# The first half batch taken unit by unit: v in q's layout, masks as bias matmuls, sink blocks of its own, and four FFN chunks between the units

## The chip, the cores and the metric

The kernel runs on one core of a Trainium2 chip. Its engines work side by side, each on its own list of instructions in a fixed order: TensorE (PE; PEld is its weight load), VectorE (DVE), ScalarE (ACT), GpSimd (POOL) and SyncE (SP), which here only issues transfers. They wait for one another through semaphores. PE writes into eight PSUM banks, P in the listings; all else works in SBUF. The metric is the device time of one execution in microseconds.

## The reference

Attention with a sliding window of 128 tokens and four sink tokens, then a feed-forward network (FFN) on its output. Inputs and output are float32; the kernel computes in bfloat16 and sums in float32.

```
B, H, S, D = 4, 8, 768, 64          # batches, heads, tokens, head size
keep = (key < 4) | ((query - key >= 0) & (query - key < 128))
a    = softmax(where(keep, q @ k.T / 8, -1e9));   o = a @ v
x    = o.transpose(0, 2, 1, 3).reshape(3072, 512)
h    = x @ w_in                     # 512 x 2048
out  = (h * sigmoid(beta * h)) @ w_out   # 2048 x 512
```

A block of 128 queries needs its own 128 keys (diagonal block, d), the 128 before them (previous block, p), and the four sink keys, which lie in key block 0 (s: a block that holds both window and sink).

## The kernel before, in words

The 3072 tokens are eight half batches of 384 (three blocks of 128). A unit is two heads of one half batch, so a half batch has four units. For a unit: q and k are cast to bfloat16 (`cast`), transposed on PE (`T`, six 128 x 128 transposes, then two copies to `qkT`), multiplied to scores (`SC`, in bursts of tiles of four blocks), put through exp on ACT into `E`, masked by multiplication on DVE or POOL, multiplied with v (`AV`; a column of ones in `vaug` gives the sum), divided by that sum (`rden`, `onorm` on DVE), and transposed into `xT` (`OT`). Query blocks from the third on do not see key block 0 through the window; for them the sink keys of all heads lie side by side in `kS`, their scores are one small matmul group (`SS`, exp to `ES`), and their values lie in `vS`, which `AV` multiplies first (line 915). For the first half batch `vS` is picked from `vaug` by a matmul with `sel` (`first_values_pe`, line 680).

A chunk of the FFN, H0 to H15 per half batch (`HQ`), is four matmuls of `w_in16` with the four units' rows of `xT` (line 970), tanh on ACT (line 975) and a product on DVE (line 977); the second layer is `OQ` (line 993). H0 and H1 need the weight tile w0, H2 and H3 w1, H4 to H7 w2 and w3, H8 to H11 w4 and w5, H12 to H15 w6 and w7. Each tile arrives as float32 (`load_w`) and is cast (`cast_w`).

The order is made in Python before anything runs. `Graph` records every operation with its reads and writes, and `arrange` then orders each engine's list by assumed durations, with PE's groups nearly in the order in which they were recorded. Where PE would stand idle in the opening, `fill` puts in matmuls of ones on ones into bank 7 (line 1212), which nobody reads. In the first half batch the recorded order is by hand, with hand-picked banks: all four units' transposes and scores, then sink scores (F) and values (V), then attention (A) and output transposes (R). The FFN of half batch 0 begins with H0 after that, between the transposes T4 to T7 of the second half batch, whose scores are the bursts S5 to S7.

Transfers go out on SP in recorded order; the first k loads go out on ACT. q and k of the first three half batches come three tokens to a partition (768-byte rows); v comes one token to a partition (256-byte rows), so that a block of v has its tokens in order. The order in which the three tokens of q and k stand is undone in the copy to `qkT`.

The lines that matter beside those: 604 (loads of q, k, v), 616 (weights), 534 to 577 (constants on POOL), 523, 525 and 528 (copies and casts on ACT, POOL and DVE), 725 (transposes), 823 (scores), 840 (exp), 848, 854 and 858 (masks), 926 (attention).

## Time and profile before

| | |
|---|---|
| Times of three runs | 221.15, 221.72 and 222.12 us, median 221.72 |
| Span of the profiled execution, first to last instruction | 219.7 us |
| Time of the profiled execution | not listed by itself; the median of the runs is 2.0 us above the span |
| PE busy | 213.4 us, 97% |
| ACT, DVE, POOL busy | 147.2, 138.1 and 75.2 us |
| Matmuls of ones on ones (line 1212) | 35, 11.3 us |
| First FFN matmul (line 970) | at 21.17 us |
| Read from memory, written | 27.37 and 6.29 MB |
| Granted TensorE clock | 1.000 |

In the page's slices each digit is the busy share in tenths of a fortieth of the span (5.5 us). In a group of instructions the figures after the bar are the busy time, the mean duration, and the idle time of the engine just ahead of them with what ended it. Durations of matmuls are modelled to the end of the array, so several in a row overlap; what counts for PE is the step from one to the next.

### The profile page before, as it was taken

The numbers are of one execution on the slowest core, as the hardware profiler recorded it, in microseconds if no ns is written. First come the engines' busy times: TensorE is split into PE (matmuls) and PEld (weight loads), VectorE is DVE, ScalarE is ACT, GpSimd is POOL, SyncE is SP. The second block draws the span as 40 slices with busy tenths as digits, with TensorE's granted clock in tenths as the row PEclk, the third lists the DMA queues.
The fourth block names the chain that finished last, engine by engine and source line by source line (L and its number), as shares of the span: only waits on it lengthen the run. The fifth ranks groups of instructions, "written<-read, shape, count | busy, mean of one in ns | idle before, by whom it ended". The sixth has DMA issues, their size and how long they took to land.

```text
span 219.7 us, 4563 instructions
## 1 busy us (share of the span) xinstructions
PE 213.4 (97%) x1776; PEld 120.8 (55%) x1793; DVE 138.1 (63%) x293; ACT 147.2 (67%) x241; POOL 75.2 (34%) x140
## 2 busy tenths in 40 slices
PE   8999999999999999999999999999999999999995
PEld 3455557555575575446554556446565456465443
DVE  1697899697774278358960788478886248088000
ACT  2698999586975798459865597275886574187211
POOL 7344551112550790067103770184101770100100
PEclk9999999999999999999999999999999999999999
DMA  6999999999989998499837997659949111400122
GB/s 190 240 302 364 357 287 357 371 298 204 226 185 188 225 141 217 92 253 218 196 74 180 228 182 203 139 142 237 136 98 209 40 63 27 144 2 0 51 95 95
DMA packets 94717, 39.86 MB, mean 181 GB/s; under 512 B 82072, under 2 KB 89512, under 8 KB 94696
## 3 DMA queue, kind: packets, MB, share of 16 engines
q1 hardware_dynamic: 91928, 33.28, 68.9%
q0 software_dynamic: 1680, 5.51, 7.5%
q10 hardware_dynamic: 1088, 0.79, 1.1%
q8 instruction: 14, 0.23, 0.5%
q14 instruction: 7, 0.06, 0.1%
HBM read 27.37 MB, written 6.29 MB: 153 GB/s over the span
## 4 chain that ended last, share of the span: by engine, by line
PE 88%; DVE 6%; DMA 3%; ACT 2%; issue 1%; ACTq 0%
PE P L993 38%; PE P L970 36%; PE P L926 5%; PE P L823 4%; DMA k_stage<-in_k_dram 3%; DVE E L858 2%; PE P L725 2%; PE P L952 1%; DVE g L977 1%; PE P L915 1%; DVE E L848 1%; PE P L870 1%; PE P L1212 1%; DVE w_in L528 1%; ACT E L840 0%
## 5 line engine op out<-in xcount | busy, mean ns | idle before, releaser
L970 PE MATMUL P<-xT,w_in 128*128 128x384 bf16 x512 | 86.8, 327 | 0.4 <-ACT w_in L523 0.2
L993 PE MATMUL P<-w_out,g 128*128 128x512 bf16 (+2 forms) x383 | 84.6, 371 | 1.0 <-issue 0.2
L975 ACT ACTIVATE t<-P,hbeta 128x384 f32<-128x384 f32 x128 | 72.4, 590 | 17.6 <-PE P L970 11.0
L977 DVE SCALAR_TENSOR_TENSOR g<-t,P 128x384 bf16<-128x384 f32 x128 | 67.9, 550 | 21.1 <-ACT t L975 15.7
L970 PEld LDWEIGHTS P<-xT,w_in 128*128 128x128 bf16 x512 | 49.0, 98 | 33.4 <-DVE g L977 0.8
L993 PEld LDWEIGHTS P<-w_out,g 128*128 128x128 bf16 x400 | 37.3, 98 | 40.5 <-issue 0.5
L840 ACT ACTIVATE E<-P 128x1024 bf16<-128x1024 f32 x44 | 43.1, 1036 | 14.1 <-PE P L823 14.1
L854 POOL TENSOR_SCALAR_AFFINE_SELECT E<-E 128x512 bf16<-128x512 bf16 x59 | 38.8, 684 | 27.4 <-ACT E L840 27.2
L1011 POOL DMA_DIRECT2D out_dram<-osb x21 | 11.8, 562 | 63.5 <-ACT osb L523 63.5
L523 ACT ACTIVATE osb<-P 128x512 f32<-128x512 f32 x14 | 8.4, 597 | 25.1 <-PE P L993 25.0
L932 DVE TENSOR_TENSOR onorm<-P,rden 128x384 bf16<-128x384 f32 x32 | 17.6, 554 | 0.8
L529 DVE TENSOR_SCALAR osb<-P 128x512 f32<-128x512 f32 x9 | 6.2, 688 | 15.0 <-PE P L993 14.9
L848 DVE TENSOR_TENSOR E<-E,maskS 128x512 bf16<-128x512 bf16 x16 | 8.8, 564 | 10.4 <-ACT E L840 10.4
L926 PE MATMUL P<-vaug,E 128*128 128x65 bf16 x352 | 15.0, 193 | 0.0
L926 PEld LDWEIGHTS P<-vaug,E 128*128 128x128 bf16 x352 | 14.0, 97 | 1.4 <-ACT E L840 0.4
L823 PEld LDWEIGHTS P<-qkT 64*128 64x128 bf16 x288 | 9.5, 94 | 7.6 <-issue 4.3
L823 PE MATMUL P<-qkT 64*128 64x128 bf16 (+1 forms) x288 | 13.2, 230 | 0.1
L1212 PE MATMUL P<-ones 128*128 128x512 bf16 (+1 forms) x35 | 11.3, 446 | 1.1 <-POOL ones L534 1.1
L528 DVE CAST vaug<-v_stage 128x512 bf16<-128x512 f32 x19 | 9.5, 509 | 3.2 <-DMA v_stage<-in_v_dram 3.1
L697 POOL TENSOR_TENSOR kS<-qkT,headm 128x8 bf16<-128x8 bf16 (+1 forms) x10 | 2.5, 251 | 17.7 <-DMA qkT<-k 9.5
L915 PE MATMUL P<-vS,ES 128*128 128x130 bf16 x40 | 8.1, 221 | 0.4 <-DVE vS L682 0.4
L525 POOL TENSOR_SCALAR_AFFINE_SELECT q<-q_stage 128x512 bf16<-128x512 f32 x7 | 4.8, 693 | 10.4 <-DMA q_stage<-in_q_dram 10.4
(64 smaller groups left out, 119.6 us busy)
## 6 DMA issues: line engine op xcount, KB each, us to landing
v_stage<-in_v_dram SPq DMA_DIRECT2D x24, 256.0 KB, 4.8
out_dram<-osb POOLq DMA_DIRECT2D x21, 256.0 KB, 3.6
q_stage<-in_q_dram SPq DMA_DIRECT2D x15, 256.0 KB, 4.8
k_stage<-in_k_dram SPq DMA_DIRECT2D x15, 256.0 KB, 4.9
wst<-in_moe_w_in_dram SPq DMA_DIRECT2D x5, 512.0 KB, 8.3
wst<-in_moe_w_out_dram SPq DMA_DIRECT2D x4, 512.0 KB, 8.1
g<-in_moe_w_out_dram SPq DMA_DIRECT2D x4, 512.0 KB, 6.6
q_stage<-in_q_dram SPq DMA_DIRECT2D x2, 768.0 KB, 7.8
```

Of the source, the lines that this page charges most:

```text
L528: return lambda e: e.tensor_copy(dst, src)
L823: add("pe", lambda e, dst=dst, kt=kt, kc=kc, rows=rows, q0=q0, nq=nq, u=u: e.matmul(dst, kt[rows, kc:kc + 128], qkT[rows, u % NT, 0, q0:q0 ...
L840: add("act", lambda e, src=src, dst_=dst_: e.activation(dst_, src, AF.Exp, bias=0.0, scale=SCALE), act_ns(1024), w=[("E", z)] + [("m", z, ...
L854: alts = {"gp": (lambda e, dd=dd, sg=sg: e.affine_select(dd, dd, [[0, 4], [sg, 128]], ALU.is_ge, 0.0, base=min(sg, 0), channel_multiplier= ...
L926: e.matmul(A[:, c0:c0 + D + 1], E[t_ % NE][:, i, hh, :], vaug[vz][:, kb % NK, 2 * hp + hh, :], start=a, stop=o, skip_group_check=True), 31,
L932: add("dve", lambda e: e.tensor_tensor(onorm[on][:, :, :, :].rearrange("p m h d -> p (m h) d"), av[:, :, 0:D], rden[on][:, :].unsqueeze(2) ...
L970: add("pe", lambda e, c=c: e.matmul(hp, w_in16[:, c, m * 128:(m + 1) * 128], xT[:, c, t0:t0 + HALF], start=(c == 0), stop=(c == 3)), mm_ns ...
L975: add("act", lambda e: e.activation(tt[ti][:, :], hp, AF.Tanh, bias=0.0, scale=hbeta[:, m:m + 1]), act_ns(HALF) + 93, r=["hbeta"], w=[("t" ...
L977: add("dve", lambda e: e.scalar_tensor_tensor(gt[T_ % NG][:, m, :], tt[ti][:, :], 1.0, hp, ALU.add, ALU.mult), dve_ns(HALF), r=[("t", ti)] ...
L993: add("pe", lambda e, m=m: e.matmul(P[:, bk, 0:n], gt[T_ % NG][:, m, t * 128:(t + 1) * 128], w_out16[:, m, cols], start=(m == 0), stop=(m ...
L1011: add(eng, lambda e: e.dma_start(out_t[3 * T_ + t], osb[z][:, :]), 262144 / 300, r=[("osb", z)], dma=f"do{eng}{z}", hold={"sp": 550, "gp": ...
L1212: G.fill([lambda e, n=n: e.matmul(P[:, 7, 0:128 * n].rearrange("p (a b) -> p a b", a=n), ones[:, :], ones[:, :].unsqueeze(1).to_broadcast( ...
```

## The change

What it does, part by part, for the first half batch only unless said otherwise:

- v is loaded like q and k, three tokens to a partition, by unit. POOL casts it into `vmix` (`mix`); nine matmuls per unit with 0/1 matrices `onehot` (`sort`) put its tokens in order into a bank, and a copy brings it to `vaug`. The 0/1 matrices are built on POOL at the start, in buffers `osb0` and `osb1`; `vmix` lies in the buffer `g1`.
- The masks are no longer multiplied into `E`. Ahead of the score matmuls, matmuls of the identity with `biasS`, `biasT` or `biasX` write 0 or -30000 into the bank, and the scores are added to that (`EARLY` is 4 in place of 0).
- Each unit has two tiles: one of four blocks (s s d d), and one of two blocks, p and a new kind x: key block 0 against query block 2 with all keys but the sink keys masked. So `SS`, `sel`, `first_values_pe` and the `vS` matmuls go for these units. `vS` for the second half batch comes from a small transfer (`load_first`) and is multiplied on POOL.
- The recorded order is by unit (`ENTRY`). H0 to H3 are computed in four parts (`HP`): as soon as a unit's `xT` is there, its one of the four matmuls of each of the four chunks is issued into four banks that stay held until the fourth unit.
- Transfers: the first loads go in the order of `LOAD0`; then come beta, w0 and w1, q and k of the second half batch, w3, w2, w5, w4, its three v tiles, w6 and w7 (`FIRST`).
- After the opening, PE's recorded order follows the string `ORDER`, with a look ahead of eight entries, in place of the rule-based choice. Banks are chosen by the planner, not by hand.
- The planner's assumed stalls and some assumed durations are changed, and an operation that may go to several engines is given, while it is recorded, to the one with the earliest free slot.

```diff
+ENTRY = "T0 S0 V0 T1 S1 V1 T2 S2 A0 A1 V2 V3 A2 R0 T3 S3 R1 P0 A3 B R2 P1 R3 P2 P3"
+FIRST = "w0 w1 q k w3 w2 w5 w4 v1 v2 v0 w6 w7"
+ORDER = "THHTTTHASHHHSHHSHAHHHAHHOROHOHHRHAHRTROHOAOHSORTOSOOATHOTHHOOHHHOSOHHOHOHRAAARAOHRROSOOHHHAHSOOHHOOHAHHRHHROHRHOROOSRAOOSOOOOHHOHAARHHHHAHOHRHHHHHHOHOOSOOHOHHOOHHSOHOHHHHHHROHHOARSAORHRAORAOOOSOAOROOHHHHHHHHROHOHHHHHHHHRHHHHHHHHOOOOOSOOOOOHHSHHHARHOOHHHHROOHOOOHOOHRRHHHOOHHOHOHOHHOOOOOOOOOOOOOOOOH"
...
+LOAD0 = "q0 k0 v0 q1 k1 v1 k3 k2 s q2 v3 v2 q3"
+LOOK, AHEAD_W = 4, 8
...
-        self.stalls = [(16000.0, 1100.0), (34000.0, 700.0)]
+        self.stalls = [(4900.0, 900.0), (14000.0, 700.0), (27000.0, 500.0), (36000.0, 500.0)]
...
-    EARLY, BST, SOON = 0, [1,2,2]+[3]*5, 2200
+    EARLY, BST, SOON = 4, [1,2,2]+[3]*5, 2200
...
+        for j in range(NK):
+            add("gp", lambda e, j=j: e.affine_select(
+                onehot[j].rearrange("p (a w) -> p a w", w=128), ones[:, :].unsqueeze(1).to_broadcast([128, NK, 128]),
+                [[-128, NK], [-1, 128]], ALU.is_equal, 0.0, base=j, channel_multiplier=NK), 520,
+                r=["ones"], w=[("pick", j), ("osb", j // 2)])
...
-        if n == "v" or hb >= CUT:
+        if n == "v" and hb == 0:
+            hs = slice(2 * i, 2 * i + 2)
+            src = v[b, hs, t0:t0 + HALF, :].rearrange("h (p j) d -> p h (j d)", j=NK)
+            dst, keys, ns = v_p[:, hs, :, :].rearrange("p h j d -> p h (j d)"), [("stv", i)], NQ0
+        elif n == "v" or hb >= CUT:
...
+    def mix(i):
+
+        hs = slice(2 * i, 2 * i + 2)
+        any_of(copies(vmix[:, hs, :], v_p[:, hs, :, :].rearrange("p h j d -> p h (j d)"),
+                      {"gp": 520}), r=[("stv", i)], w=[("vmix", i)], lock=True)
+
+    def sort(i):
+
+        G.begin()
+        bk = take(1)
+        hs = slice(2 * i, 2 * i + 2)
+        for c in range(NK):
+            for j in range(NK):
+                add("pe", lambda e, c=c, j=j: e.matmul(
+                    P[:, bk[0], 128 * c:128 * c + 128], onehot[j][:, c * 128:(c + 1) * 128], vmix[:, hs, j * D:(j + 1) * D],
+                    start=j == 0, stop=j == NK - 1), mm_ns(128), r=[("pick", j), ("osb", j // 2), ("vmix", i)],
+                    x=[("B", bk[0])])
+        any_of(copies(vaug[0][:, :, hs, 0:D], P[:, bk[0], 0:HALF].rearrange("p (c h d) -> p c h d", h=2, d=D),
+                      {"act": 380, "dve": 465}),
+               r=[("vones", 0)], w=[("v", 0, c, i) for c in range(NK)], x=[("B", bk[0])])
+        give(bk)
...
-        add("dve", lambda e: e.tensor_tensor(
+        add("dve" if b else "gp", lambda e: e.tensor_tensor(
             vS[z][:, :, 0:D], vS32[:, 0:1, :].to_broadcast([128, H, D]),
...
+        if hb == 0:
+            return [t for i in range(4) for t in (
+                [("s", i, 0, 0), ("s", i, 0, 1), ("d", i, 1, 1), ("d", i, 2, 2)], [("p", i, 1, 2), ("x", i, 0, 2)])]
...
+                               "px": [(0, biasPX)]}[kinds]:
+                    dst = bank[:, a:min(a + 2, len(kinds)), :]
+                    add("pe", lambda e, dst=dst, src=src, a=a: e.matmul(
+                        dst, ident[:, :], src, start=a == 0, stop=False, skip_group_check=True), mm_ns(128 * min(2, len(kinds))),
...
-            far = NK * half + m >= 2
+            far = NK * half + m >= 2 and u >= EARLY
...
+    def HP(c):
+        G.begin()
+        if c == 0:
+            for m in range(4):
+                first_h.extend(take(1))
+        for m in range(4):
+            HQ(0, m, [first_h[m]], [c])
...
-    for x in "T0:63 T1:01 S1:01 T2:64 T3:46 S0:12 S4:56 S3:34 S2:01 F:2 V:5 A1:1 A0:5 A2:4 R0:5 A3:2 R1:0 R2:4 R3:0".split():
...
+    for x in ENTRY.split():
+        i = int(x[1:] or 0)
+        if x[0] == "V":
+            sort(i)
...
+        elif x[0] == "P":
+            HP(i)
+            if i == 3:
+                give(first_h)
...
-    early = "H0 T4 H1 H2 H3 T5 H4 T6 T7 H5 S5 H6 H7 H8 H9 S6 H10 H11 S7 H12 H13 H14".split()
...
+    todo, idle_ = list(ORDER), 0
     while True:
         background()
         now = G.free["pe"]
+        if todo:
...
+            for pos, x in enumerate(todo[:AHEAD_W + 4 * max(0, idle_ - 8)]):
```

In the letters of the orders, T is a transpose group, S a score burst, V a sort, A attention, R an output transpose, P a quarter of H0 to H3, B beta, H a chunk, O a quarter of a second-layer tile.

More of the change, by code (lines that the diff above doesn't have):

```diff
@@ L214, in arrange @@
                     t = max(self.free[e], ready(o, e), self.shut(o, e))
[L215 removed]
+                    if o.dma and o.chain != 0:
                         t = max(t, self.dma_free - 3000)
@@ L603, in load @@
         after = [("stg", n, z, j) for j in range(4)] if hb in range(CUT, CUT + NSTG) and n != "v" else ()
+        if hb == 2 and n == "v":
+            after = [("stv", j) for j in range(4)]
         add("act" if hb == 0 and n == "k" and Q2 else "sp", lambda e: e.dma_start(dst, src), ns, w=keys,
@@ L645, in cast @@
             r, w = [("stb", n, z, i), ("vones", hb % NV)], [("v", hb % NV, i)]
+            w += [("v", 0, i, j) for j in range(4)] if hb == NV else []
         elif hb == 0:
@@ L790, in SC @@
         tiles, first = BURSTS[n]
+        assert all(t_ < NE or SPAN[t_ - NE][1] < done["AV"] for t_ in tiles)
         bs = take(2 * len(tiles))
@@ L973, in HQ @@
                 r=w_keys(m) + [("xT", c, T_ % NXT)], x=[("B", bs[0])])
-        spare_ = [("wst", NWS // 2 + z) for z in range(NWS // 2)] if (T_, m) == (NG - 1, 0) else []
+        if cs[-1] < 3:
+            return
+        ti = hi[0] % NTT
+        hi[0] += 1
+        spare_ = [("vmix", i) for i in range(4)] if T_ == 1 and m < 4 else []
+        spare_ += [("wst", NWS // 2 + z) for z in range(NWS // 2)] if (T_, m) == (NG - 1, 0) else []
         add("act", lambda e: e.activation(tt[ti][:, :], hp, AF.Tanh, bias=0.0, scale=hbeta[:, m:m + 1]),
```

254 lines of the change are left out of this document (143 added, 111 removed).

## The prediction

> **What bounds the kernel now.** I read the page first (who is busy, and in which slices), then the sums by stretch, then the chain of work in order of time, then the timeline of the first 37 us. The page:
>
> ```profile
> span 219.7 us, 4563 instructions
> PE 213.4 (97%) x1776; PEld 120.8 (55%) x1793; DVE 138.1 (63%) x293; ACT 147.2 (67%) x241; POOL 75.2 (34%) x140
> ...
> PE   8999999999999999999999999999999999999995
> ...
> L1212 PE MATMUL P<-ones 128*128 128x512 bf16 (+1 forms) x35 | 11.3, 446 | 1.1 <-POOL ones L534 1.1
> ```
>
> PE is nearly always busy, but 11.3 us of that are L1212, matmuls of ones on ones that nobody reads. All of them lie in the opening, so only the opening has PE time to give. The busy time by stretch (start:end, length, then PE, PEld, DVE, ACT, POOL, clock, DMA share, GB/s):
>
> ```profile
> 5.30:21.20 15.90, 14.32 (x163) 8.36 (x162) 12.56 (x31) 12.74 (x23) 6.50 (x18) 1.00 1.06 298
> 21.20:24.20 3.00, 3.00 (x24) 1.77 (x24) 1.68 (x4) 2.67 (x6) 2.30 (x3) 1.00 1.04 386
> 24.20:36.40 12.20, 11.94 (x150) 7.66 (x150) 12.04 (x27) 12.13 (x21) 5.09 (x6) 1.00 1.06 319
> 36.40:217.30 180.90, 179.86 (x1440) 101.56 (x1453) 110.96 (x232) 117.88 (x192) 57.31 (x94) 1.00 0.74 159
> ```
>
> After 36.4 PE runs 179.86 of 180.90 us: the change must deliver PE to this stretch earlier, or it delivers nothing. In 24.2 to 36.4 DVE and ACT are full as well. The chain there (start, length, what):
>
> ```profile
> 22.96 1.31 PE P L970 x8
> ...
> 24.91 0.56 DVE g L977
> 25.47 0.60 DVE w_in L528
> 26.07 0.67 DVE E L858 x2
> ...
> 31.45 2.77 PE P L970 x16
> ```
>
> It runs over DVE: gate products, weight casts and masks hold PE's banks. The transfers (columns as above) slow down where the 256-byte rows of v pass, 8 to 12 us, and every weight waits in the same line:
>
> ```profile
> 6.00:8.00 2.00, 1.58 (x13) 0.88 (x11) 0.75 (x2) 1.23 (x3) 0.49 (x3) 1.00 1.06 292
> 8.00:10.00 2.00, 2.00 (x20) 0.96 (x18) 1.55 (x4) 1.36 (x2) 0.92 (x5) 1.00 1.13 205
> 10.00:12.00 2.00, 1.91 (x26) 1.05 (x26) 1.95 (x5) 1.70 (x4) 1.38 (x4) 1.00 0.87 171
> ```
>
> The timeline, last, gives the prices:
>
> ```profile
> 5.31 0.53 PE L725 MATMUL P<-ident,q 128*128 128x128 bf16 x3
> 6.99 0.33 PE L725 MATMUL P<-ident,q 128*128 128x128 bf16 x3
> 24.00 1.05 POOL L525 TENSOR_SCALAR_AFFINE_SELECT w_in<-g 128x1024 bf16<-128x1024 f32 x1 [0.30 <-DMA g<-in_moe_w_in_dram]
> 24.20 0.62 PE L823 MATMUL P<-qkT 64*128 64x256 bf16 x14
> 30.77 1.05 POOL L525 TENSOR_SCALAR_AFFINE_SELECT w_in<-wst 128x1024 bf16<-128x1024 f32 x1 [1.57 <-DMA wst<-in_moe_w_in_dram]
> ```
>
> The bracket names the landing that ended the wait: w3 lands at 24.00, w7 at 30.77. Three transposes take 0.53 us at 5.31 and 0.33 at 6.99, of which some 0.2 is the end's latency: the array steps at half rate before about 6.5 us, with PE busy since 1.06.
>
> **The change part by part.** I compare one state in both kernels: first FFN chunks H0 to H3 and transposes T4 to T7 done. Before reaches it at 24.20, where the next score burst starts.
>
> *Loads.* v's 786 KB move at about 190 GB/s (205 and 171) before; in 768-byte rows, as q and k, at about 290: 4.1 against 2.7 us, so the line gains 1.4 us for all behind it (bounds 0.4, if it reaches only 212 GB/s, and 1.8 at the 340 that the stretch from 12 to 18 us moves). w0 and w1 pass q and k of the second half batch: 2.36 MB at 290 from 2 us on end near 10, a weight's 0.5 MB at 340 takes 1.5: w0 (before 19.16) lands near 12, w1 near 14. Those q and k, cast at 15.21 and 17.62 before, move by two weights (1.34 each, by the weight casts at 22.66 and 24.00) to 15.21 + 2.7 - 1.4 = 16.5 and 18.9; T4 needs them at 22, so that costs nothing. w3 and w2 keep their place: 24.0 - 1.4 = 22.6, plus the 1.05 cast: H4 from 23.7. Two v tiles (262 KB each at the 219 to 301 GB/s of 26 to 32 us, about 1.0 us) pass w7: 30.8 + 2.0 - 1.4 = 31.4, cast by 32.4.
>
> *PE's opening.* The constants' new order on POOL puts ones behind kS (0.20), two bias triangles (0.54) and biasS (0.41): PE starts 1.2 us later, near 2.3, and seven fillers at 0.43 and one at 0.21 precede T0, at 5.5 (before 5.31). If the full rate again comes 5.4 us after the start, it comes at 7.7, and T0 (0.64) and the first unit's six bias matmuls run at half rate. No row has a bias matmul; a 512-column filler steps 0.43 cold and 0.22 warm, so 256 columns are 0.21 or 0.11: PE is through them at 7.7.
>
> The page "TensorE: Matmul & The Clock Gate" of the Trainium skill (Part 1) speaks against this part: activity releases the half rate in a window of about 3.4 us that runs freely, so the full rate could come, as an estimate, anywhere from 5.7 to 9.1 us here. By its late end the opening would lose some 0.7 us more; the trace's one switch at 6.5 fits.
>
> From 7.7 PE executes in a fixed order, by warm rows: four score bursts of ten (0.33 each, by 0.11 for a pair of 256 columns and 0.056 for 128) 1.3; eighteen bias matmuls 1.95; 36 sort matmuls at 0.056 2.0; T1 to T3 1.0; 72 attention matmuls at 0.03 2.2; twelve output transposes 0.7; sixteen FFN matmuls at 0.163 (0.65 per four) 2.6; six fillers of 512 and seven of 256 columns 2.05; switching after score bursts 4 x 0.13 (0.77 for a dense burst of three tiles against 0.64) 0.5. Sum 14.3: chunk H3 ends near 22.0. T4 to T7 add 1.36. The four chunks hold four of eight banks until ACT's tanh (0.58) and DVE's product (0.55) of each; T6 and T7 want those banks, some 1.0 late. State reached: 24.4. Bounds: 22.9 (no bank wait, early full rate) and 26.0 (late full rate, slow POOL).
>
> *What else moves.* Removed from DVE: seven masks (0.42), three v casts (0.42), vS0 (0.68), 4.9 us; added: three copies of sorted v, nearest row the 384-column copy from P at 0.56, 1.7. None of it bounds the opening, as PE now does. ACT: four exps of 1024 columns and four of 512 replace five and a small one. The 512 form is between 0.49 (384 columns) and 1.03; I take 0.60, nearer the lower; with a v copy ACT gains 1.5 us, under cover while PE is busy to 22. POOL: three one-hot blocks and four mixes of 384 columns, between 0.41 (256) and 0.65 (512), taken 0.53, 3.7 us, and vS0, between 0.25 (8 columns of that operation) and 1.05 (1024 of a cast), taken 1.0; first read by the second half batch's attention near 30. Queued behind it are the casts of w0 (0.62) and w1 (1.06), needed at 18; POOL is through with them near 15.6, so 2.4 us cover it; without that cover its whole price shows.
>
> *Second stretch.* 24.20 to 36.4 holds eleven chunks (7.15), three bursts (1.65), sink scores (0.17), twelve attention blocks (2.16): 11.1 of 12.2 us, 1.1 lost to waits. After, the work is the same. The first weights are cast earlier; H12 needs w7 (32.4), and PE arrives at 24.4 + 8 chunks 5.2 + bursts 1.8 + half the attention 1.1 = 32.5, just in time. I take 0.6 of waits (bounds 0 and 1.6).
>
> Sum: +0.2 in the state, -0.5 in waits: span 219.7 - 0.3 = 219.4. The shown runs' median is 2.0 above the span, and I put that around it again: **221.4 us**. From bounds: -2.5 and +2.3.
>
> **The rivals.**
>
> *Faster: the opening is not held by banks.* H3 ends at 22.0, T7 at 23.4, H4 starts on w2's cast at 23.7, and DVE's 3.2 us of relief removes the second stretch's waits: -0.8 - 1.1 = -1.9, **219.8 us**. For it: the chain over DVE from 24.91 to 31.4. Against: ACT stays as full as DVE there.
>
> *Slower: POOL and DVE slow each other.* POOL gets 4.7 us more between 5 and 16, beside DVE's casts. A k cast took 0.52 beside POOL against 0.43 for q casts, a POOL mask 0.82 at 10.80 beside DVE against 0.63: 0.09 on eight casts and 0.2 on four mixes are 1.5 us if all lie on PE's order. It decides once sort matmuls wait for mixes; each mix has about 2 us of room. Then **222.9 us**. The page "GPSIMD Engine Reference" of the Trainium skill (8. Key points) has a rule for it: POOL shares its SBUF interfaces with DVE, and two-port modes contend. The two pairs of rows agree, but could have other causes.
>
> *Slower: w7 is late.* If the line gains 0.4 instead of 1.4, w7 is cast by 33.4, 0.9 after PE wants it, and the weights behind it are as late: +1.2 with the waits that follow, **222.6 to 223**. Against: the 292 GB/s row beside 171.
>
> **How the numbers follow.** A measurement of this kernel tells about 0.5% (1.1 us) from no change. My case (within 1.1 us of before) 0.42; the faster rival 0.34; contention 0.14 and the late w7 0.10, together 0.24 for slower. The range leaves out about a tenth at each end: 219.3 (past the faster rival, short of the bound 219.2) to 223.6 (past both slower ones); my case's own is 220.6 to 222.8.
>
> **What would show it.** Right: H0 starts near 18, H3 ends near 22, T7 near 24.4; w0's cast is done before 15; the bias matmuls step 0.11; after 37 the stretches look alike; fillers fall from 11.3 us to about 6, and PE's real work grows by 4, none of it FFN. Wrong: H4 after 25.5 (slower) or before 23.8 with S5 directly behind (faster); a PE wait for POOL's mix; H12 waiting for the cast of wst; gaps on PE after 40, which I have as none in both.

## The result: the changed kernel is 0.9% slower

The changed kernel takes 223.46 us (median of 8, 222.52 to 224.31), the kernel before, run beside it, 221.56 us. The ratio is 1.0091 with a 95% interval of 1.0066 to 1.0116, some 2.0 us; one execution of the kernel before, at 227.35 us in a slower state, is left out of it. The profiled execution of the changed kernel is the slowest of its eight (224.31), so its profile shows about 0.9 us more loss than the median.

The page of the changed kernel:

```profile
span 222.6 us, 4681 instructions
...
PE 215.0 (97%) x1847; PEld 123.7 (56%) x1847; DVE 132.8 (60%) x286; ACT 149.8 (67%) x248; POOL 74.3 (33%) x139
...
PE   5999898999999999999999999999999999999995
...
L1301 PE MATMUL P<-ones 128*128 128x512 bf16 (+1 forms) x22 | 7.5, 429 | 2.5 <-POOL ones L576 2.5
```

The matmuls that nobody reads fall from 35 to 22, as they should, and the span is still 2.9 us longer. Three states that both kernels pass say where:

| state | before | after | added |
|---|---|---|---|
| H0 to H3 and T4 to T7 done | 24.20 | 24.93 | 0.73 |
| H16 starts (H0 to H15, A4 to A7 and the first 20 output matmuls done) | 42.01 | 44.45 | 1.71 |
| last matmul ends | 217.25 | 220.08 | 0.39 |

All three rows compare single profiled executions, and the opening's share moves with the clock by half a microsecond and more (last section). The sums by stretch of the changed kernel (start:end, length, then PE, PEld, DVE, ACT, POOL, clock, DMA share, GB/s), the last one up to the start of H16:

```profile
5.30:21.20 15.90, 15.90 (x211) 11.85 (x210) 10.05 (x26) 10.72 (x19) 8.08 (x26) 1.00 1.08 341
21.20:24.20 3.00, 2.31 (x25) 1.49 (x24) 1.65 (x4) 3.00 (x8) 2.46 (x3) 1.00 1.14 338
24.20:36.40 12.20, 11.26 (x129) 6.95 (x128) 11.43 (x26) 12.06 (x21) 4.02 (x6) 1.00 0.99 299
21.20:44.45 23.25, 20.93 (x216) 12.46 (x215) 21.06 (x44) 19.34 (x35) 8.77 (x10) 1.00 1.02 324
```

and the kernel before up to its start of H16:

```profile
21.20:42.01 20.81, 20.49 (x205) 12.42 (x207) 18.64 (x43) 18.27 (x31) 8.44 (x9) 1.00 1.05 345
```

Read the third figure behind the comma, DVE. Up to 21.2 us VectorE falls from 12.56 to 10.05 us, and PE gains nothing from it: it is busy in all 15.90 us. From there to H16 VectorE rises from 18.64 to 21.06. By tile, it casts four tiles of w_out there (3.00 us) in place of two (1.36) and copies three qkT (1.57) in place of one (0.75). That looks like work moved from one stretch into the other, but neither is on VectorE's part of the path to H16. The copies end at 25.9, and VectorE later waits for an exp; the last two casts stand behind the last normalised unit (onorm) that H16 needs:

```profile
29.90 0.42 DVE L931 TENSOR_TENSOR E<-E,osb 128x512 bf16<-128x512 bf16 x1 [0.53 <-ACT E L913]
...
42.80 0.56 DVE L1006 TENSOR_TENSOR onorm<-P,rden 128x384 bf16<-128x384 f32 x1
43.27 1.28 DVE L570 CAST w_out<-wst 128x1024 bf16<-128x1024 f32 x2
```

ScalarE takes 1.1 us more from 21.2 to H16, as much as its qkT copies grow (2.15 in place of 1.07), and up to 29.9 the chain of waits runs mostly over ScalarE.

The chain of waits of the changed kernel there, in order of time (start, length, what):

```profile
29.90 0.42 DVE E L931
...
32.96 1.04 DVE w_in L570
34.00 1.39 DVE g L1065 x3
...
36.06 1.07 DVE w_out L570
37.13 1.18 DVE E L931
...
42.06 0.60 DVE w_out L570
...
42.80 0.57 DVE onorm L1006
...
44.62 0.49 PE P L1053 x3
```

VectorE carries it from 29.9 to 43.4 without a break, up to that last onorm. From H4 (24.93) to H16 PE is without a matmul for 1.47 us, the kernel before from 24.20 to its H16 for 0.32; the three longest of these waits are for VectorE:

```profile
34.06 0.82 PE L1053 MATMUL P<-xT,w_in 128*128 128x384 bf16 x4 [0.52 <-DVE w_in L570]
38.37 0.26 PE L1000 MATMUL P<-vaug,E 128*128 128x65 bf16 x3 [0.40 <-DVE E L931]
42.12 0.34 PE L1026 MATMUL P<-ident,onorm 128*128 128x128 bf16 x3 [0.19 <-DVE onorm L1006]
```

Some of VectorE's steps are far too long. The timeline of VectorE and GpSimd at that place (start, length, engine, line, operation):

```profile
35.95 0.64 POOL L927 TENSOR_SCALAR_AFFINE_SELECT E<-E 128x512 bf16<-128x512 bf16 x1 [2.49 <-ACT E L913]
35.99 1.15 DVE L570 CAST w_out<-wst 128x1024 bf16<-128x1024 f32 x1
36.99 1.05 POOL L567 TENSOR_SCALAR_AFFINE_SELECT w_out<-g 128x1024 bf16<-128x1024 f32 x1 [0.40 <-DMA g<-in_moe_w_out_dram]
37.05 1.26 DVE L931 TENSOR_TENSOR E<-E,osb 128x512 bf16<-128x512 bf16 x1
...
38.34 1.05 POOL L567 TENSOR_SCALAR_AFFINE_SELECT w_out<-g 128x1024 bf16<-128x1024 f32 x1 [0.30 <-DMA g<-in_moe_w_out_dram]
38.92 0.74 DVE L931 TENSOR_TENSOR E<-E,osb 128x512 bf16<-128x512 bf16 x1
```

A mask that takes 0.42 at 29.90 takes 1.26 when it starts 0.06 us behind a GpSimd cast, and ends 0.27 us behind that cast's end; the mask at 38.92, beside the next GpSimd cast, takes 0.74, and a w_out cast 1.15 in place of 0.68. With the w_in cast at 32.88 (1.12, and 0.68 undisturbed) these four are some 2.1 us too long; in the kernel before, two masks of 0.85 make 0.9.

The opening's loss is at T6 and T7 (PE's timeline):

```profile
24.09 0.34 PE L795 MATMUL P<-ident,k 128*128 128x128 bf16 x3 [0.59 <-DVE g L1065]
24.27 0.33 PE L795 MATMUL P<-ident,q 128*128 128x128 bf16 x3
24.75 0.34 PE L795 MATMUL P<-ident,k 128*128 128x128 bf16 x3 [0.15 <-ACT qkT L565]
```

The first of these waits is for a bank that the early chunks hold until VectorE's product g, as forecast, the last for a copy of qkT on ScalarE. The 0.39 us of the rest include one wait of 0.32 at 61.97, for g behind an exp, a mask and a k cast.

### The profile page after: what moved, and what is told of

It is laid out like the page before. It is cut to its first block, busy times and chain, and to the rows that moved or that the text cites. A ratio compares the mean times of both kernels' runs of the same rounds, so it can differ in the third digit from the quotient of the medians.

```text
span 222.6 us, 4681 instructions
## 1 busy us (share of the span) xinstructions
PE 215.0 (97%) x1847; PEld 123.7 (56%) x1847; DVE 132.8 (60%) x286; ACT 149.8 (67%) x248; POOL 74.3 (33%) x139
## 4 chain that ended last, share of the span: by engine, by line
PE 86%; DVE 7%; ACT 4%; POOL 1%; issue 1%; POOLq 0%
PE P L1081 36%; PE P L1053 34%; PE P L1000 4%; PE P L895 4%; PE P L1301 2%; DVE g L1065 2%; ACT E L913 2%; DVE E L931 2%; PE P L876 1%; PE P L795 1%; ACT t L1063 1%; PE P L705 1%; DVE onorm L1006 1%; PE P L1026 1%; DVE w_out L570 1%; ACT qkT L565 1%
## 5 line engine op out<-in xcount | busy, mean ns | idle before, releaser
L1053 PE MATMUL P<-xT,w_in 128*128 128x384 bf16 x512 | 91.7, 326 | 1.1 <-DVE w_in L570 0.5
L1081 PE MATMUL P<-w_out,g 128*128 128x512 bf16 (+2 forms) x400 | 91.0, 371 | 0.0
L913 ACT ACTIVATE E<-P 128x1024 bf16<-128x1024 f32 (+1 forms) x47 | 44.0, 999 | 5.7 <-PE P L895 5.5
L565 ACT ACTIVATE osb<-P 128x512 f32<-128x512 f32 x20 | 11.9, 597 | 20.7 <-PE P L1081 20.6
L1006 DVE TENSOR_TENSOR onorm<-P,rden 128x384 bf16<-128x384 f32 x32 | 17.5, 553 | 0.7
L570 DVE CAST q<-q_stage 128x512 bf16<-128x512 f32 (+1 forms) x18 | 7.4, 432 | 6.5 <-DMA q_stage<-in_q_dram 6.5
L570 DVE CAST vaug<-v_stage 128x512 bf16<-128x512 f32 x16 | 7.6, 475 | 6.0 <-DMA v_stage<-in_v_dram 6.0
L1301 PE MATMUL P<-ones 128*128 128x512 bf16 (+1 forms) x22 | 7.5, 429 | 2.5 <-POOL ones L576 2.5
L565 ACT ACTIVATE qkT<-P 128x384 bf16<-128x384 bf16 (+1 forms) x12 | 6.5, 584 | 2.9 <-PE P L795 2.8
L1004 DVE RECIPROCAL rden<-P 128x6 f32<-128x6 f32 x32 | 5.8, 187 | 4.5 <-PE P L1000 4.3
L565 ACT ACTIVATE xT<-P 128x384 bf16<-128x384 bf16 x10 | 5.0, 503 | 4.2 <-PE P L1026 4.2
```

The lines of the kernel that those rows point to most:

```text
L565: return lambda e: e.activation(dst, src, AF.Copy, bias=0.0, scale=scale)
L570: return lambda e: e.tensor_copy(dst, src)
L913: add("act", lambda e, src=src, dst_=dst_: e.activation(dst_, src, AF.Exp, bias=0.0, scale=SCALE), act_ns(256 * ns_), w=[("E", z)] + [("m" ...
L1006: add("dve", lambda e: e.tensor_tensor(onorm[on][:, :, :, :].rearrange("p m h d -> p (m h) d"), av[:, :, 0:D], rden[on][:, :].unsqueeze(2) ...
L1053: add("pe", lambda e, c=c: e.matmul(hp, w_in16[:, c, m * 128:(m + 1) * 128], xT[:, c, t0:t0 + HALF], start=(c == 0), stop=(c == 3)), mm_ns ...
L1081: add("pe", lambda e, m=m: e.matmul(P[:, bk, 0:n], gt[T_ % NG][:, m, t * 128:(t + 1) * 128], w_out16[:, m, cols], start=(m == 0), stop=(m ...
```

## The experiments

All were timed in rounds beside the kernel before. The ratio is to that; the other columns come from one profile each: start of H4, start of H16, and the time between the two.

| run | median us | ratio, 95% interval | H4 | H16 | between |
|---|---|---|---|---|---|
| before | 221.56 | 1 | 25.15 | 42.01 | 16.86 |
| changed | 223.46 | 1.0091 (1.0066 to 1.0116) | 24.93 | 44.45 | 19.53 |
| v_rows_2k | 223.89 | 1.0094 (1.0065 to 1.0123) | 24.09 | 43.64 | 19.56 |
| weights_then_v | 224.72 | 1.0124 (1.0087 to 1.0160) | 24.96 | 44.77 | 19.81 |
| no_unit_ffn | 225.43 | 1.0165 (1.0125 to 1.0205) | 24.75 | 46.16 | 21.41 |
| before_unit_ffn | 227.42 | 1.0247 (1.0216 to 1.0277) | 25.79 | 43.43 | 17.64 |
| scores_early | 223.93 | 1.0113 (1.0083 to 1.0143) | 27.04 | 45.19 | 18.15 |
| qk_ahead_of_w | 227.72 | 1.0298 (1.0264 to 1.0331) | 24.57 | 46.75 | 22.19 |
| before_w_ahead | 223.40 | 1.0093 (1.0063 to 1.0124) | 26.24 | 43.92 | 17.68 |
| small_pool_work | 223.62 | 1.0088 (1.0059 to 1.0117) | 25.27 | 43.63 | 18.37 |
| t_ahead_of_h | 226.09 | 1.0202 (1.0169 to 1.0236) | 23.96 | 45.99 | 22.03 |
| t_ahead_w_early | 228.95 | 1.0309 (1.0273 to 1.0345) | 26.37 | 48.26 | 21.89 |
| no_written_order | 228.27 | 1.0275 (1.0222 to 1.0328) | 24.56 | 45.39 | 20.83 |
| small_pool_masks | 223.17 | 1.0061 (1.0037 to 1.0086) | 23.91 | 42.33 | 18.42 |
| small_dve_casts | 223.06 | 1.0077 (1.0046 to 1.0108) | 24.93 | 43.28 | 18.35 |
| small_dve_and_masks | 222.98 | 1.0073 (1.0048 to 1.0098) | 25.22 | 43.98 | 18.76 |
| ones_on_dve | 222.89 | 1.0072 (1.0042 to 1.0102) | 24.56 | 43.04 | 18.48 |
| w_out_off_dve | 223.19 | 1.0101 (1.0051 to 1.0152) | 24.79 | 42.77 | 17.97 |
| v_part_alone | 225.68 | 1.0183 (1.0160 to 1.0206) | 26.81 | 45.06 | 18.25 |
| v_part_alone_ones | 225.44 | 1.0166 (1.0139 to 1.0194) | 27.36 | 46.87 | 19.51 |

H4 and H16 can only be set against each other where the order of PE's work is the same; scores_early, no_unit_ffn, qk_ahead_of_w, no_written_order, the two with T ahead, the two with the v part alone, and the kernels built on before have other work on the other side of H4 or H16.

**Is w7 late?** It lands at 32.61 (forecast 31.4, before 30.7), and H12 waits 0.52 for its cast. The SP queue is held for 8.87 us at the three v tiles ahead of w6 and w7, and the transfers sink to 167 GB/s from 24 to 26 us.

```diff
-            src = v[0, :, t0 + i * 128:t0 + (i + 1) * 128, :].rearrange("h p d -> p h d")        # second half batch
+            src = v[0].rearrange("h t d -> (h t d)")[(3 + i) * 65536:(4 + i) * 65536].rearrange("(p x) -> p x", p=128)
```

> The changed kernel, the order of all engines and queues as it is; only the three v tiles of the second half batch are read as contiguous rows of 2048 bytes (the same bytes in all, other tokens, so this kernel multiplies wrong values of v) in place of rows of 256 bytes. Theory L (the loss after 25 us is the late w6 and w7, held up by the v tiles ahead of them in the line): the SP queue's wait of 8.87 us at 16.05 shrinks to under 6, w6 lands near 29.5 and w7 near 31.2 (30.99 and 32.61 in the changed kernel), H12 does not wait for the cast of wst, and the time falls by 0.8 to 1.3 us. Rival D (VectorE and ScalarE are full there whatever lands): w7 lands as early, but H12 or the chunks behind it wait for other work of VectorE instead, and the time falls by less than 0.4 us.

Measured: w7 lands at 29.73, earlier than expected, and nothing comes of it, as rival D has it. The time is the same and so is the stretch from H4, 19.56 us. PE's timeline shows why:

```profile
33.44 0.82 PE L1053 MATMUL P<-xT,w_in 128*128 128x384 bf16 x4 [0.46 <-DVE w_in L570]
```

H12 still waits for the cast, which begins at 32.70, three microseconds after the landing: it stands behind an attention unit's onorm and a mask in VectorE's order. The theory of the late weights falls.

```diff
-FIRST = "w0 w1 q k w3 w2 w5 w4 v1 v2 v0 w6 w7"
+FIRST = "w0 w1 q k w3 w2 w5 w4 w6 w7 v1 v2 v0"
```

> The changed kernel with w6 and w7 loaded ahead of the three v tiles of the second half batch, as they nearly stood before; the planner lays the rest out again. Theory L: w7 lands near 29.5, H12 no longer waits, the v tiles land near 32.5 and are in time for the attention of the second half batch only if that moves behind more FFN chunks; 0.5 to 1.3 us faster than the changed kernel. Rival D: within 0.4 us of it, or slower if the attention of the second half batch now waits for v.

It is no faster either. v now lands at 28.66 to 30.64. H12 no longer waits for its weights, but PE waits for VectorE's products all the same, 0.77 us at 30.78 and 1.02 at 34.52, the second behind two v casts of 0.86 and 0.85 (0.42 undisturbed) and a mask of 1.26, and H16 is as late as in the changed kernel.

**The parts, done or undone one at a time.** The order of the loads alone, in the kernel before:

```diff
-    LOADS = xl(0) + x1[0:1] + x1[1:2] + [0] + [1] + [2] + ...
+    LOADS = xl(0) + [0] + [1] + x1[0:1] + x1[1:2] + [2] + ...
```

> The kernel before with w0 and w1 loaded ahead of q and k of the second half batch, and nothing else (no FFN chunk by unit). Theory S: k lands some 2.5 us later than before, the first burst of the second half batch starts at 25.5 or later instead of 24.2, H16 starts 1 to 1.5 us later than 42.01, and the kernel is 0.8 to 2.0 us slower than before. Rival: T4 to T7 wait for PE and banks anyway, q and k late cost nothing, within 0.5 us of before.

This one line costs the kernel before as much as the whole change costs: 0.93%. VectorE and PE in its timeline:

```profile
21.40 0.76 DVE L528 CAST k<-k_stage 128x512 bf16<-128x512 f32 x2 [0.78 <-DMA k_stage<-in_k_dram]
...
24.28 0.34 PE L725 MATMUL P<-ident,q 128*128 128x128 bf16 x3 [0.26 <-DVE qkT L528]
```

VectorE waits 0.78 us for k (landed at 21.38, before 17.56), and then has k's casts, the products of H0 to H3 and the qkT copies all at once; T4 starts at 22.20 in place of 19.47, and H16 is 1.9 us late. Of the expected figures the time holds; k is 3.8 us later (2.5 expected), H16 more than 1.5, and the first burst, expected at 25.5 or later, starts at 24.77.

```diff
-A3:2 R1:0 R2:4 R3:0
+A3:2 R1:0 B:1 P0:3654 R2:1 P1 R3:0 P2 P3      # P: one contraction block of H0 to H3; w0 and w1 ahead as above
```

> The kernel before with one part of the change alone: w0 and w1 loaded ahead of q and k of the second half batch, and H0 to H3 run by unit, one contraction block as soon as its unit is transposed; v, the masks, the constants and the order of the other loads stay as before. Theory V (the part that costs is v's: 60 bias and one-hot matmuls of 5.6 us on PE, and the v tiles ahead of w6 and w7): this kernel has the gain without them and is 1.0 to 2.5 us faster than before. Rival F (the opening gains nothing from early chunks, since v lands last and units are through only near 21 us): within 0.6 us of before.

Slower than the load order alone, and outside both expectations. H16 starts at 43.43, 1.4 us late. The other 3.9 us come behind 43 us, where the rule that chooses the remaining work laid it out anew (bursts waiting 0.5 to 0.75 us for exps around 93 and 118 us), so the total says nothing of the early chunks. That H16 is not early although H0 starts at 18.77 speaks for rival F.

```diff
-ENTRY = "... S3 R1 P0 A3 B R2 P1 R3 P2 P3"
+ENTRY = "... S3 R1 A3 B R2 R3"                # and H0 to H3 whole, between T4 and T5
```

> The changed kernel without the four FFN chunks by unit: H0 to H3 run as whole chunks between the transposes T4 and T5, as before. Theory B (holding four banks costs what the early chunks gain): T4 to T7 run without a wait for a bank, fillers grow by some 2.5 us, H4 starts within 0.5 us of 24.93, and the time is within 0.5 us of the changed kernel. Rival E (the early chunks are the part that earns): H4 starts at 26 or later, and the kernel is 1.0 to 2.0 us slower than the changed one.

In the changed kernel, on the other hand, the early chunks earn: without them it is 0.7% slower still, 2 us, at the top of rival E's range (by T7, which ends at 26.4, not by H4, which runs ahead of T6). Theory B falls. How much of the 2 us is the chunks' stays open: its profile has 3.1 us of drawn-out VectorE instructions from H4 to H16, against 2.1 in the changed kernel.

```diff
-FIRST = "w0 w1 q k w3 w2 ..."
+FIRST = "q k w0 w1 w3 w2 ..."
```

> The changed kernel with q and k of the second half batch loaded ahead of w0 and w1, as before. Theory S: k lands near 16.7 in place of 19.6, T4 to T7 can go earlier, but w0 lands near 18 and the early FFN chunks wait for it with fillers in their place; the planner puts the bursts of the second half batch directly behind T7, and H16 starts 0.5 to 1.5 us earlier, the time falls by as much. Rival E (the early chunks earn, and they need w0 early): H4 starts later than 25.5 and the kernel is 0.5 to 2.0 us slower than the changed one.

Rival E's side, beyond its figure: w0 lands at 17.17 and w1 at 19.51, 14 fillers run where the changed kernel runs two, H0 starts at 20.03 and T7 ends near 28 (H4, at 24.57, runs ahead of T5).

```diff
-FIRST = "w0 w1 q k w3 w2 w5 w4 v1 v2 v0 w6 w7"
+FIRST = "q k w0 w1 w3 w2 w5 w4 w6 v2 w7 v1 v0"
-ENTRY = "... S3 R1 P0 A3 B R2 P1 R3 P2 P3"
+ENTRY = "... S3 R1 A3 B R2 R3"
-ORDER = "THHTTTHASHHHSHHSHAHHHA..."
+ORDER = "TTHHTTSHHHHSHHHHSHHHHHAAAH..."
```

> The v part of the change alone: v in rows of 768 bytes with the one-hot ordering, bias masks and own sink blocks stay; H0 to H3 run as whole chunks behind T4 and T5, q and k of the second half batch are loaded ahead of w0 and w1 and the v tiles among w6 and w7 as before, and the second stretch is written in the order that the kernel before has. Theory W (the load order and the early chunks cost, the v part is about free, as PE has fillers to give): T4 starts by 20, T7 ends near 23.5, H16 at 42 to 43, within 0.8 us of before. Rival V (the v part costs, by 5.6 us of matmuls and a late full clock): T4 not before 21, H16 at 44 or later, 1.5 to 3 us slower than before.

1.8% slower. Theory W falls, but rival V's mechanism isn't what is seen: T4 starts at 20.0, only 0.5 us later than before. The time goes where T6 and T7 wait 1.10 us for VectorE's product and 0.42 for a copy on ScalarE, and in one wait of 1.42 us at 31.93 for VectorE, behind a v cast of 0.85 and a mask of 0.86. So the parts don't add up: each order of the work gives its own waits.

```diff
-        add("gp", lambda e: e.memset(ones[:, :], 1.0), 150, w=["ones"])
+        add("dve", lambda e: e.memset(ones[:, :], 1.0), 150, w=["ones"])
```

> The same with the ones set by VectorE, so that PE starts near 1.1 as in the kernel before. Theory W with P (the later start costs some 0.5 us): 0.3 to 0.7 us faster than the run beside it, and level with before or up to 0.5 us faster. Rival: within 0.3 us of the run beside it.

0.24 us faster than the run beside it, inside both intervals: no gain shown.

**The order of the second stretch.**

```diff
-ORDER = "THHTTTHASHHHSHHSHAHHHA..."
+ORDER = "TTTTSHHHSHHHSHHHAHHAHA..."
```

> The changed kernel, only the written order of the second stretch altered: the three score bursts of the second half batch come directly behind T4 to T7 (SHHHSHHHS) in place of behind three, five and eight FFN chunks. The run with v in 2 KB rows had w7 1.9 us before H12 started and gained nothing, so theory L is given up. Theory S (a chain sets the end of the stretch: T4 to T7, the bursts, their exps on ScalarE and masks on VectorE, attention A4 to A7, the transposes, H16; its first burst starts at 27.0 against 24.2 before): the bursts start near 25, 27 and 29, A7 ends 1 to 2 us earlier, H16 starts near 43 (44.45), and the kernel is 1.0 to 2.0 us faster than the changed one. Rival D (VectorE's work, 21.2 us of 23.3, sets it, whatever comes first): H16 within 0.6 us of 44.45, the time within 0.5 us of the changed kernel.

The bursts start at 26.1, 28.4 and 30.4 in place of 27.0, 29.2 and 32.9. The attention then comes later all the same (first unit at 36.1), H16 at 45.19. Theory S falls: PE lost what the bursts gained in four waits for VectorE's products and ScalarE's exps ahead of 33.5 us (the longest 0.72), and ran without a wait from there.

```diff
-ENTRY = "... S3 R1 P0 A3 B R2 P1 R3 P2 P3"
+ENTRY = "... S3 R1 T4 A3 B T5 R2 T6 R3 T7 P0 P1 P2 P3"
-FIRST = "w0 w1 q k ..."
+FIRST = "q k w0 w1 ..."
```

> The changed kernel with T4 to T7 moved ahead of the FFN chunks by unit, q and k of the second half batch loaded ahead of w0 and w1 (as before), and the bursts at the front of the second stretch. The kernel before with w0 and w1 ahead of q and k alone was as slow as the changed kernel, and its H16 started 1.9 us late. Theory K (late q and k put T4 to T7 and their eight copies, 0.5 us each, into the stretch where VectorE and ScalarE are full, and these cannot catch up): T7 ends near 22, H3 near 24.5, the first burst starts by 25, H16 at 42 to 43, and the kernel is 1.5 to 2.5 us faster than the changed one, level with before. Rival D (the sum of VectorE's work to H16 is what counts, wherever T4 to T7 stand): H16 after 44, within 0.6 us of the changed kernel. Rival E (early chunks earn): w0 late, H16 after 45, slower.

T7 ends at 21.2, 3.9 us earlier than in the changed kernel, and the kernel is 1.1% slower than the changed one. The planner put six chunks ahead of the first burst (25.4), and the end of the stretch is a cast that waits for its weights, in VectorE's order ahead of the last onorm, for which PE stands idle 1.58 us (the chain):

```profile
35.40 8.07 DMA wst<-in_moe_w_out_dram
...
43.50 0.69 DVE w_out L570
...
44.33 0.57 DVE onorm L1006
```

So theory K, that late transposes of the second half batch are the cause, is not borne out in the changed kernel, though this run's own wait keeps it from being a clean test. In the kernel before the load order does cost; what of it is the transposes was not tested.

```diff
+ENTRY = "... S3 R1 T4 P0 A3 B T5 R2 P1 T6 R3 P2 T7 P3"        # FIRST as in the changed kernel
```

> The same move of T4 to T7, but w0 and w1 stay ahead of q and k in the line, as in the changed kernel. Theory K: q and k land at 16.4 and 19.5 as there, PE waits for them or runs fillers (some 20 in place of 7 from 16 to 20 us), T7 ends near 23.5, so only part of the gain: H16 at 43.5 to 44.5, 0 to 1 us faster than the changed kernel. If q and k's landing is not what counts, it is level with the run that loads them first.

PE waits behind q and k with 13 fillers at 17.5, and T7 ends near 25.8; slower than the run that loads q and k first, as theory K has it for that pair, but slower than the changed kernel too, which it did not expect.

```diff
-ORDER = "THHTTTHASHHHSHHSHAHH..."
+ORDER = ""
```

> The changed kernel with an empty written order: behind H3 the rule of the kernel before chooses the next piece of work. Theory K or D (VectorE and ScalarE set the second stretch): H16 is a bad mark here, as the rule puts other chunks ahead; the time is within 1.5 us of the changed kernel on either side. Rival O (the written order is what costs): 1.5 to 2.5 us faster, level with before.

The rule of the kernel before does worse with this opening than the written order, by 1.8%, which neither side expected. Rival O falls.

**Work taken out of the second stretch, orders unchanged.**

```diff
-    dd, dd, [[0, 4], [sg, 128]], ALU.is_ge, ...
+    dd[:, :, 0:8], dd[:, :, 0:8], [[0, 4], [sg, 8]], ALU.is_ge, ...          # GpSimd, units 4 to 7
-    copies(dst, src_, {"gp": 1060})
+    copies(dst[:, :, 0:8], src_[:, :, 0:8], {"gp": 1060})                    # GpSimd, w_out
```

> The changed kernel with all orders as they are; on GpSimd only, the masks of the second half batch cover 8 of 128 columns and two casts of w_out (35 to 40 us) 8 of 512 columns of each row block, the rest left undone (that part of w_out is zero, set by VectorE before its first cast). Theory C (a VectorE operation that meets one of GpSimd waits it out): the mask of 1.26 us at 37.05 and that of 0.74 at 38.92 return to 0.42, the w_out cast of 1.15 to 0.68 and the w_in cast of 1.12 at 32.88 to 0.68, 2.0 us together on a chain that runs over VectorE from 29.9 to 43.4; H16 starts 1.0 to 2.0 us earlier and the time falls by 0.8 to 1.8. Rival: the durations return, but the chain moves to ScalarE's exps, and the time falls by less than 0.4 us.

The stretch falls to 18.37 us, 1.16 less, as theory C has it. The time does not show it: H4 is at 25.27, with the full clock near 8.3 us in place of 7.5. The clearing of w_out on VectorE (1.56 us at 0.98) need not be the reason: scores_early has no clearing, and its H0 is nearly as late (18.39 against 18.46, and 18.12 in the changed kernel). The masks alone, without that clearing:

> The changed kernel with all orders as they are; GpSimd's three masks of the second half batch cover 8 of 128 columns, the rest is left unmasked. Theory C (VectorE waits out what GpSimd runs beside it): the w_in cast of 1.12 us at 32.88 returns to 0.68, the w_out cast at 35.99 from 1.15 to 0.7 or stays where it meets GpSimd's cast; the stretch from H4 to H16, 19.52 us, is 0.4 to 1.0 us shorter and the time 0.3 to 1.0 us less. Rival: durations return, the stretch is as long, since ScalarE's exps set it.

(Of the diff above, only the first pair of lines.) 18.42 us, and a ratio of 1.0061: 0.3% under the changed kernel's, with intervals that overlap. From H4 to H16 no cast of VectorE takes over 0.72 us in its profile and no mask over 0.51, so theory C's durations do return. The stretch doesn't fall by all of their 2.1 us because the opening is a microsecond early there and the weights hardly: VectorE waits 0.70 us at 24.89 and 0.32 at 32.04 for tiles of w_in. The same for VectorE's casts:

```diff
-    copies(dst, src_, {"dve": 602})
+    copies(dst[:, :, 0:8], src_[:, :, 0:8], {"dve": 602})                    # VectorE, four tiles of w_out
```

> The changed kernel with all orders as they are; the four casts of w_out that VectorE has between 36 and 45 us cover 8 of 512 columns of each row block, the rest of those tiles is left zero (set before VectorE's first cast). Theory D (VectorE's sum of work sets the stretch from H4 to H16): 1.15 us less at 35.99 and 0.67 less at 41.99 come off the chain, H4 to H16 takes 17.8 to 18.5 in place of 19.52 us, and the time falls by 0.8 to 1.6 us. Rival A (ScalarE, 16.3 of 20 us busy there, or the landing of weights takes its place): H4 to H16 at 19 or more, the time within 0.5 us of the changed kernel.

> Both cuts in one kernel, all orders as they are: VectorE's four casts of w_out on 8 of 512 columns and GpSimd's three masks of the second half batch on 8 of 128 (both left undone otherwise). Theory D: the gains add, 1.1 us of the masks' run and 1.2 of the casts', H4 to H16 near 17.2, the time 1.5 to 2.5 us below the changed kernel, level with before. Rival A: no more than the run with the masks alone, H4 to H16 at 18.2 to 18.6.

(The second has this diff and the masks'.) 18.35 us for the casts, as theory D expected, but in the same profile the mask of 1.26 us is at 0.42, so the run does not separate the casts from the meetings. Both together give 18.76: they don't add; a v cast that took 0.42 takes 1.27 there, and PE waits 0.74 us for it. In time the two are 0.1 and 0.2% under the changed kernel, far from theory D's figures.

```diff
-    {"act": 947, "dve": 602, "gp": 1060}
+    {"act": 947, "gp": 1060} if j >= 8 else {"act": 947, "dve": 602, "gp": 1060}
```

> The changed kernel with VectorE taken from the engines that may cast w_out, so that ScalarE and GpSimd do all eight; nothing left out, the order of PE is the same up to H28. Theory D: VectorE is relieved of 2.9 us before H16, of which some 1.2 lie on the chain, and the time falls by 0.6 to 1.5 us, unless GpSimd's longer casts (1.05 us each) slow VectorE as its masks did: then by less than 0.4. Rival A: ScalarE becomes the bound, 0 to 1.5 us slower.

With nothing left out and the same order on PE, the stretch is 17.97 us (sums by stretch, columns as above):

```profile
24.79:42.77 17.98, 17.59 (x187) 10.59 (x186) 15.44 (x38) 16.74 (x28) 7.06 (x8) 1.00 0.99 329
```

VectorE is at 15.44, ScalarE at 16.74, and PE is idle for 0.39 us, against 1.47 in the changed kernel (18.05 of 19.52) and 0.32 in the kernel before (17.49 of 17.81 from 24.20 to 42.01). That is the strongest sign that VectorE set the stretch. It does not say by which of its instructions: besides the casts taken off, only one of the others, a mask of 0.85, is still drawn out, so the stretch also lost 1.2 us of meetings. The profiled execution gains what theory D expected; the median, with two of six times at 225.5, is 0.3 us lower, the ratio, 1.0101, is not lower at all, and its interval takes in both theories.

**PE's later start.**

> The changed kernel with one constant, the ones that the fillers and the identity are made from, set by VectorE (idle until 3.9 us) instead of GpSimd; PE's order is the same but for two more fillers ahead of T0. Theory P (the later start costs): PE starts near 1.1 instead of 2.46, the full clock comes 1.0 to 1.5 us earlier on the average, at half rate a us later costs half a us of PE's work, H0 starts at 17.3 to 17.8 (18.12), and the time falls by 0.4 to 0.8 us. Rival: the clock changes at a time that does not follow PE's start, or H4 waits for T4 to T7 anyway; within 0.3 us of the changed kernel.

```diff
-        add("gp", lambda e: e.memset(ones[:, :], 1.0), 150, w=["ones"])
+        add("dve", lambda e: e.memset(ones[:, :], 1.0), 150, w=["ones"])
```

PE starts at 1.12 and H0 at 17.76; 0.2% under the changed kernel, in theory P's range, with overlapping intervals. Its reason isn't borne out: PE starts 1.34 us earlier, the full clock comes only some 0.45 us earlier, and between the two runs of the v part alone, with the same change, it comes 1.0 us later (7.05 in place of 6.0). Its second stretch is the better find. The order of every engine there is the changed kernel's, and it takes 18.48 us, as short as with the masks left out:

```profile
35.59 1.20 POOL L927 TENSOR_SCALAR_AFFINE_SELECT E<-E 128x512 bf16<-128x512 bf16 x1 [2.50 <-ACT E L913]
35.62 0.68 DVE L570 CAST w_out<-wst 128x1024 bf16<-128x1024 f32 x1
36.22 0.85 DVE L931 TENSOR_TENSOR E<-E,osb 128x512 bf16<-128x512 bf16 x1
...
37.68 0.57 DVE L931 TENSOR_TENSOR E<-E,osb 128x512 bf16<-128x512 bf16 x1
```

Here GpSimd's mask is the one that is drawn out (1.20 in place of 0.64), VectorE's cast runs in 0.68, and its mask is under way before GpSimd's cast begins at 36.75. Counted from H4, the two profiles put every VectorE instruction up to that cast at the same time to 0.01 us. Then three of its instructions are shorter, the cast by 0.46, the masks by 0.41 and 0.17, together 1.04 us, and H16 is 1.05 us earlier. The same instructions in the same order meet or miss each other by some tenths of a microsecond, and that is what the 1.05 us are. So 1.0 of the 1.71 us that the profile of the changed kernel loses in this stretch are such meetings, and the gains of the smaller kernels above in their profiles are of that size too: what they are worth beyond it is not shown. Without it the stretch is still 0.7 us longer than the 17.81 of before. Much of that is one more meeting: the w_in cast, beside a GpSimd mask, takes 1.12 us here too, and H12 waits 0.51 for it; where it takes 0.69 (w_out_off_dve) H12 waits less than 0.1.

## Why the prediction was wrong

- **The opening: the path right, one wait too small.** w0 and w1 landed at 12.46 and 13.99 (12 and 14), PE started at 2.46 (2.3), the full rate came at 7.5 (7.7), H0 at 18.12 (18), H3 ended at 22.2 (22.0), fillers took 7.5 us (6). PE never waited for GpSimd's mix. T6 and T7 waited for banks as said, but from H3's end to the state it took 2.7 us where the forecast had 1.36 and some 1.0. The state came at 24.93, 0.73 late where the forecast had 0.2, and inside its bounds (22.9 to 26.0).
- **The step that failed: "I take 0.6 of waits", and with it "-0.5 in waits" for the second stretch.** The half microsecond was not there to win: the row that shows the stretch before has PE busy in 11.94 of 12.20 us, so it stood idle for 0.26, and the rest of the "1.1 lost to waits" is what the price list left out. And nothing was put for VectorE's own instructions getting longer, in a stretch where its row was full (12.04 of 12.20). In place of -0.5 the stretch gave +1.7 in the profile: PE's idle time rose from 0.32 to 1.47 us, most of it in waits for VectorE, whose casts and masks beside GpSimd ran 2.1 us over their usual time. Of the 1.7 us, 1.05 went with the same orders in ones_on_dve, where they ran 1.0 over, and nearly all in w_out_off_dve (17.97 against 17.81 of before), where they ran 0.4 over. VectorE's relief in the opening, 2.5 us by the sums, gave PE nothing.
- **"Those q and k ... so that costs nothing":** in the kernel before this move alone costs 0.93%. The sentence asked when PE wants T4, not when VectorE and ScalarE can do the casts and copies that k releases. In the changed kernel T4 and T5 run without a wait, and the move's share couldn't be isolated: putting q and k back makes the early chunks late.
- **"gaps on PE after 40, which I have as none":** two short ones at 42.1 and 43.4, behind the same chain of VectorE, one of 0.32 us at 61.97, and 0.39 us for all behind H16.
- **The rivals.** The slow rival of contention had the right mechanism at the wrong place: not in the opening, where mixes have room, but on VectorE's chain from 33 to 39 us. The rule of the Trainium skill's "GPSIMD Engine Reference" (8. Key points), that GpSimd shares its SBUF interfaces with VectorE, agrees with the mask of 1.26 us in place of 0.42 beside GpSimd's cast. The late w7 gave its sign (H12 waits for the cast) and was not the cause: the sign stays when w7 lands 2.9 us earlier. The faster rival gave VectorE's relief the whole 1.1 us of waits, and falls by the same 0.26.
- **A slip in the sums.** The lower bounds, -1.3 in the state and -1.1 in waits, add up to -2.4 and not -2.5; nothing hangs on it.
- **What stays open.** The cause is shown for the profile of the changed kernel, which is its slowest execution, and not for the medians. By the profiles the opening costs from -0.3 to 1.1 us, as the full clock comes early or late in kernels of the same order, the second stretch 0.2 to 1.8 and the rest 0.4; but no single change gives back more than 0.3% of the time, with intervals that overlap, also where the profile's second stretch is nearly as short as before. No version here beats the kernel before. That the forecast's range, up to 223.6, takes in 223.46 is owed to its two slower rivals, and neither is what was seen; the sum itself had two terms too small by 0.5 and 2.2 us in the profile.

## What to carry to other kernels

Sum a stretch on every engine that is nearly full in it, not only on the one that the page calls the bound: work taken off an engine where PE hides it is no gain, and where an engine's list is full, every instruction of it that runs longer than usual reaches PE. Before a stretch is credited with waits that will go, read from its row how long the bound engine really stands idle there. Ask of an earlier or later load not only when its consumer wants it, but how many casts and copies it sets free at once and on which engine. And before a difference of a microsecond between two profiles is explained, look whether it lies in pairs of VectorE and GpSimd instructions that may as well have missed each other.

## What the runs showed of the hardware

The time of the full clock varies more than was allowed for. PE is busy with fillers from its first matmul in all of these kernels, and the full rate came between 2.7 us (before_w_ahead, 1.07 to 3.74) and 5.9 us (ones_on_dve, 1.12 to 7.05) after it. The first unit's six bias matmuls of the changed kernel, and of v_rows_2k, whose orders are the same:

```profile
6.49 1.32 PE L876 MATMUL P<-osb,ident 128*128 128x256 bf16 x6
```

```profile
6.15 0.82 PE L876 MATMUL P<-osb,ident 128*128 128x256 bf16 x6
```

In the second the full rate came between 5.6 and 6.0 us in place of 7.5, and everything up to T7 came 0.84 us earlier (H4 at 24.09 for 24.93). Over the profiles of kernels that share the changed kernel's order up to T7, H4 started between 23.9 (small_pool_masks, full rate near 5.4) and 25.3 (small_pool_work, near 8.3), some half a microsecond later for each microsecond at half rate. The page "TensorE: Matmul & The Clock Gate" of the Trainium skill (Part 1) has a freely running window of about 3.4 us and a change that varies by half a microsecond either way for it; the traces here have it vary by 3.2 us, the 2.7 is less than one such window, and the traces decide. So two single profiles of this kernel can differ by more than a microsecond before anything has changed.
